# Grams three tiles behind the keys, first gate/up chunks column-tiled, attention state masked one chunk at a time

## The chip, the cores and the metric

The kernel runs on one core of one Trainium2 chip. The metric is the device time of one execution in microseconds (us); lower is better. Three runs of the kernel before gave 291.62, 291.98 and 292.02 us, with a median of 291.98 us. The profile is that of one more execution (291.88 us), whose recorded span is 290.6 us. TensorE had its full clock throughout (granted clock 1.0).

The engines are called as in the profile: PE is TensorE (matmuls), PEld its weight loads, DVE is VectorE, ACT is ScalarE, POOL is GpSimd, SP is SyncE, which here issues transfers.

## The reference

Two branches read the same input x of 2048 tokens by 640 channels, and a gate of one number per token mixes them. Branch A is linear attention with 32 heads of 20 channels and a feature map of two softmaxes; branch B is a gated feed-forward layer of width 1728.

```python
qkv = (x @ wqkv)                                   # then split into q, k, v by head
pq, pk = q @ w_phi, k @ w_phi                      # per head, 20x20
phi_q = concat([softmax(pq), softmax(-pq)])        # 40 features per head
phi_k = concat([softmax(pk), softmax(-pk)])
kv  = einsum("bhsf,bhsd->bhfd", phi_k, v)          # the state: sum over all 2048 tokens
z   = einsum("bhsf->bhf", phi_k)
num = einsum("bhqf,bhfd->bhqd", phi_q, kv)
den = einsum("bhqf,bhf->bhq", phi_q, z)[..., None] + 1e-6
a   = (num / den) @ wo
b   = (gelu(x @ w_gate) * (x @ w_up)) @ w_down
g   = sigmoid((x * gate_w).sum(-1, keepdims=True))
out = g * a + (1 - g) * b
```

## The kernel before

The tokens are handled as 16 tiles of 128 and as 4 blocks of 512. The kernel has two stages.

In the first stage, each tile's values and keys (`vk`, in tiles 4 to 7 the keys alone) are multiplied out into PSUM. ScalarE takes the exponentials (`k_evac`, lines 413 and 416 of the profile), VectorE normalises them into softmaxes (`k_norm`: a sum at line 424, a reciprocal at line 428, two multiplications at line 433), and TensorE then adds the tile's part of the state (`gram`, line 449). Normalised keys lie in a ring of four slots. In between, TensorE multiplies out the queries (`pq`), whose exponentials are at line 516.

TensorE's array can be used as one piece (128 columns of weights) or as two column halves that work side by side. `mm` writes either form, by the flag `self.columns`; line 351 of the profile is the matmul in it. The grams always use the halves.

```python
def mm(self, bank, c0, n, lhs, rhs, first, fin, reads):
    for a, z in ((0, 64), (64, P)) if self.columns else ((0, P),):
        self.sc.op("pe", lambda e: e.matmul(
            self.ps[a:z, bank * 512 + c0:bank * 512 + c0 + n], lhs[:, a:z], rhs, start=first, stop=fin),
            reads=reads, writes=[("ps", bank)], signal=fin and z == P)
...
# end of attention_state (self.columns is True here)
for t in range(4, NT):
    if t < 8:
        self.k_early(t, 1)
    else:
        self.vk(t)
    self.k_norm(t)
    m = 2 * t - 2 if t < 8 else t + 5
    while n < m:
        if n == m - 1:
            for g in range(g, t - 2 if t < 8 else t - 1):
                self.gram(g)
            g = t - 2 if t < 8 else t - 1
        self.pq(order[n][0], order[n][1], n)
        n += 1
```

The second stage is the feed-forward layer with the rest of the attention among it. For a block of 512 tokens, `gateup` makes one of 14 chunks of the hidden layer: five matmuls for the gate into one PSUM bank, five for the up projection into another (line 620), a gelu on ScalarE (line 623), and a product on VectorE (`hT`, line 625), which frees the second bank. Chunks alternate between the bank pairs (0, 1) and (6, 7). The remainder chunk, number 13, packs its 64 gate and 64 up columns into one group of five matmuls (line 630) and uses one bank.

After the first three chunks of the first block come the last two grams. The state is copied out of PSUM (`kv_evac`), turned by a transfer (line 475), and masked to its block-diagonal form by 20 small products on VectorE (`kv_mask`, line 504), after 4 small copies (line 485). `num(t)` then multiplies a tile's queries with the state into banks 2 to 5 (line 653) and divides on VectorE (lines 669 to 680, the last of which read those banks). `down_pair` makes the output projection in steps of two matmuls that use the two row halves of the array (line 710).

```python
def gateups(b, after):
    for idx, c in enumerate([0, 1, 13] + list(range(2, 13))):
        if c == 13:
            self.gateup(b, c, (2,))
        else:
            self.gateup(b, c, pairs[self.pn % 2])
            self.pn += 1
        after(idx)

def downs(b, side):
    ...                      # the steps of down_pair; before step n:
    if n in side:
        self.num(side[n])

def state(idx):
    if idx == 2:
        self.gram(14)
        self.gram(15)
        self.kv_evac()
        self.gates()
    if idx == 6:
        self.kv_mask()

def first_nums(idx):
    if idx in (3, 6, 9, 12):
        self.num(idx // 3 - 1)
...
at = (8, 44, 80, 116)
gateups(0, state)
gateups(1, first_nums)
for b in range(self.NB):
    downs(b, {at[k]: 4 * b + 4 + k for k in range(4)} if b < 3 else {})
    if b < 2:
        gateups(b + 2, none)
```

Waits are placed by a small scheduler: every instruction waits for the last writer and readers of the buffers that it names, and each engine runs its instructions in the order in which the program issues them.

Of the kernel before, what the change touches and what calls it, by code (L numbers as in the profile page):

```python
# [3 lines left out]
P = 128  # L4
# [3 lines left out]
ALU = mybir.AluOpType  # L8
# [99 lines left out]
class _Kernel:  # L108
# [368 lines left out]
            self.Ek[:, 0, :, :].rearrange("p s f -> p (s f)")),  # L477
            reads=[("Ek", 0, 0), ("Ek", 0, 1)], writes=[("Ek", 2, 0), ("Ek", 2, 1)])

    def kv_mask(self):  # L480
        sc = self.sc
        for r in (0, 1):
            for s in (0, 1):
                a, z = 64 * r, 64 * r + 64
                sc.op("dve", lambda e: e.tensor_copy(
                    self.KV[a:z, :, s, :].rearrange("p i (h c) -> p i h c", c=self.DB)[:, :, :, self.DB - 1],
                    self.hmask[a:z, r, :, :]), reads=[("hmask", r)], writes=[("KVd", r, s)])
        self.kvk = {(i, r): [] for i in range(self.KD) for r in (0, 1)}
        lows = {g: lo for g, a, b, c, lo, f0, nf in self.gram_groups()}
        for i in range(self.KD):  # L490
            for r in (0, 1):
                j = 5 * r + i
                a, q = 64 * r, 64 * (j % 2)
                hlo = 16 * r + 3 * i
                for g in range(hlo // 3, (hlo + 3) // 3 + 1):
                    h0, h1 = max(hlo, 3 * g), min(hlo + 3, 3 * g + 2)
                    nh, j0 = h1 - h0 + 1, h0 - hlo
                    o = (j // 2) * P + 64 * (g % 2) + h0 * self.DA - lows[g]
                    dst = self.KV[a:a + 64, i, :, j0 * self.DB:(j0 + nh) * self.DB].rearrange(
                        "p s (h c) -> p s h c", c=self.DB)[:, :, :, 0:self.DA]  # L500
                    src = self.Ek[q:q + 64, 2, :, o:o + nh * self.DA].rearrange("p s (h c) -> p s h c", c=self.DA)
                    m = self.hmask[q:q + 64, j % 2, i, j0:j0 + nh].unsqueeze(1).unsqueeze(3).to_broadcast(
                        [64, 2, nh, self.DA])
                    sc.op("dve", lambda e: e.tensor_tensor(dst, src, m, ALU.mult),  # L504
                          reads=[("Ek", 2, 0), ("hmask", j % 2), ("KVd", r, 0), ("KVd", r, 1)],
                          writes=[("KV", i, r, g)])
                    self.kvk[i, r].append(("KV", i, r, g))

    def pq(self, b, i, n):
        sc = self.sc  # L510
# [19 lines left out]
    def attention_state(self):  # L530
        NT = self.NT
        order = [(b, i) for b in range(self.NB) for i in range(self.KD)]
        sc = self.sc
        sc.op("dve", lambda e: e.memset(self.zero[:, :], 0.0), writes=["zero"])

        def warm(n):
            for i in range(n):
                sc.op("pe", lambda e: e.matmul(self.bank(0), self.zero[:, 0:P], self.zero[:, :], start=True, stop=True),
                      reads=["zero"], writes=[("ps", 0)])
        vs, ve, xt = self.v_step, self.v_first_evac, self.x_transpose  # L540
        warm(7)
        xt(0, 6, "d")
        xt(1, 7, "a")
        xt(2, 2, "d")
        xt(3, 3, "a")
        for t in range(4):
            vs(t, 0)
        for t in range(4):
            vs(t, 1)
        for t in range(4):  # L550
            vs(t, 2)
        for t in range(4):
            vs(t, 3)
        self.blockdiag()
        self.gate_column(6)
        for t in range(4):
            vs(t, 4)
            ve([t], "ad"[t % 2], False)
            if t == 2:
                ve([0, 1, 2], "a", True)  # L560
        ve([3], "d", True)
        f = self.fold
        self.v_early(4, 6)
        self.v_early(5, 0)
        f(0, "k", (2, 3), "d")
        f(1, "k", (4, 5), "a")
        self.v_early(6, 6)
        f(2, "k", (2, 3), "d")
        f(3, "k", (4, 5), "a")
        f(4, "k", (0, 1), "d")  # L570
        self.v_early(7, 6)
        self.k_early(0, 2)
        f(0, "q", (4, 5), "d")
        f(1, "q", (6, 7), "d")
        self.k_early(1, 0)
        f(2, "q", (4, 5), "d")
        f(3, "q", (6, 7), "d")
        self.k_early(2, 2)
        f(4, "q", (4, 5), "d")
        self.k_norm(0)  # L580
        self.k_early(3, 0)
        self.k_norm(1)
        self.pq(0, 1, 1)
        self.pq(0, 0, 0)
        self.pq(0, 3, 3)
        self.columns = True
        self.gram(0)
        self.k_norm(2)
        self.pq(0, 2, 2)
        self.k_norm(3)  # L590
        n = 4
        g = 1
# [6 lines that stand above are left out]
            m = 2 * t - 2 if t < 8 else t + 5  # L599
            while n < m:  # L600
                if n == m - 1:
                    for g in range(g, t - 2 if t < 8 else t - 1):
                        self.gram(g)
                    g = t - 2 if t < 8 else t - 1
                self.pq(order[n][0], order[n][1], n)
                n += 1

    def gateup(self, b, c, banks):
        sc = self.sc
        xs = lambda kt: self.xT[:, kt, b * self.BT:(b + 1) * self.BT]  # L610
        xr = [("xT", t) for t in range(4 * b, 4 * b + 4)]
# [4 lines left out]
        if c < 13:  # L616
            i = 0 if c < 7 else 1
            for w, wk, bk in ((self.wg_sb, "wg", banks[0]), (self.wu_sb, "wu", banks[1])):
                for kt in range(self.KD):
                    sc.op("pe", lambda e, kt=kt, w=w, bk=bk: e.matmul(  # L620
                        self.bank(bk), w[:, kt, c * P:(c + 1) * P], xs(kt), start=(kt == 0), stop=(kt == self.KD - 1)),
                        reads=xr + [(wk, i)], writes=[("ps", bk)], signal=(kt == self.KD - 1))
            sc.op("act", lambda e: e.activation(self.gl[:, slot, :], self.bank(banks[0]), AF.Gelu_apprx_tanh),  # L623
                  reads=[("ps", banks[0])], writes=[("gl", slot)], guard=self.oldw)
            sc.op("dve", lambda e: e.tensor_tensor(hT[:, c, :], self.bank(banks[1]), self.gl[:, slot, :], ALU.mult),  # L625
                  reads=[("ps", banks[1]), ("gl", slot)], writes=[("hT", hk, c)], guard=oldw)
        else:
            bk = banks[0]
            for kt in range(self.KD):
                sc.op("pe", lambda e, kt=kt: e.matmul(  # L630
                    self.bank(bk), self.wgu_sb[:, kt, :], xs(kt), start=(kt == 0), stop=(kt == self.KD - 1)),
                    reads=xr + ["wgu0", "wgu1"], writes=[("ps", bk)], signal=(kt == self.KD - 1))
            sc.op("act", lambda e: e.activation(self.gl[64:128, slot, :], self.ps[0:64, bk * 512:bk * 512 + 512],
                                                AF.Gelu_apprx_tanh),
                  reads=[("ps", bk)], writes=[("gl", slot)], guard=self.oldw)
            for r in (0, 1):
                odd = lambda v: v.rearrange("p (u r q) -> p u r q", r=2, q=P)[:, :, r, :]
                sc.op("dve", lambda e: e.tensor_tensor(
                    odd(hT[64 * r:64 * r + 64, c, :]), odd(self.ps[64:128, bk * 512:bk * 512 + 512]),
                    odd(self.gl[64:128, slot, :]), ALU.mult),  # L640
                    reads=[("ps", bk), ("gl", slot)], writes=[("hT", hk, c, r)], guard=oldw)
# [110 lines left out]
    def ffn(self):  # L752
        self.gn = 0
        self.pn = 0
        self.columns = False
        pairs = [(0, 1), (6, 7)]

        def gateups(b, after):
            for idx, c in enumerate([0, 1, 13] + list(range(2, 13))):
                if c == 13:  # L760
                    self.gateup(b, c, (2,))
                else:
                    self.gateup(b, c, pairs[self.pn % 2])
                    self.pn += 1
                after(idx)

        def downs(b, side):
# [7 lines left out]
                        self.num(side[n])  # L775

        def state(idx):
            if idx == 2:
                self.gram(14)
                self.gram(15)  # L780
                self.kv_evac()
                self.gates()
            if idx == 6:
                self.kv_mask()

        def first_nums(idx):
            if idx in (3, 6, 9, 12):
                self.num(idx // 3 - 1)

        def none(idx):  # L790
            pass
        at = (8, 44, 80, 116)
        gateups(0, state)
        gateups(1, first_nums)
        for b in range(self.NB):
# [47 lines left out]
```

The softmax here doesn't subtract the row's maximum and nothing guards it: scores larger than these inputs give would overflow.

## Time and profile before

| what | value |
|---|---|
| time, median of 3 | 291.98 us |
| span of the profile | 290.6 us |
| gate/up matmuls (line 620) | 506 recorded, 379 ns each as recorded, overlapping |
| down and output projection (line 710) | 1258 recorded, 93.6 us |
| products hT (line 625) | 52, 691 ns each |
| gelu (line 623) | 52, 598 ns each |
| normalising one tile: lines 424, 428, 433 | 1481 + 553 + 2 x 822 ns |
| mask products (line 504) | 20, 189 to 290 ns each |

A line of the waits reads: engine and line that waited, the engine and line whose end released it, then the total in us, how often, and the longest. A line of the timeline reads: start in us, length in us, engine, line, operation, output and inputs, and how many instructions are merged in it; in brackets the idle time of the engine before it and what ended that. Successive matmuls overlap in the records, since their ends are modelled, so the pace of TensorE is read from starts, and a few matmul records are missing.

### The profile page before, as it was taken

How to read it: one execution, taken by the hardware profiler on the slowest of the kernel's cores; microseconds unless marked ns; L12 is line 12 of the kernel's file. 1: busy time of each engine (PE TensorE's matmuls, PEld its weight loads, DVE VectorE, ACT ScalarE, POOL GpSimd, SP SyncE). 2: the span in 40 equal slices, each digit the busy share in tenths (PEclk: the TensorE clock that was granted, in tenths of full speed). 3: DMA queues.
4: the chain of work that ended last, by engine and by line, in shares of the span. 5: the costliest groups of instructions: out<-in, count | busy, mean ns of one | idle time of the engine just before them, and what ended most of it. 6: DMA issues, size and time to landing. Idle time of an engine off the chain costs nothing.

```text
span 290.6 us, 6966 instructions
## 1 busy us (share of the span) xinstructions
PE 282.1 (97%) x2990; PEld 179.2 (62%) x3007; DVE 167.5 (58%) x337; ACT 105.2 (36%) x199; POOL 27.6 (10%) x52
## 2 busy tenths in 40 slices
PE   7999998999999999999999999999999999999996
PEld 3666788699954444444477644447764444777786
DVE  2248999999876742677767533235753323575001
ACT  3367887576673223222202232320223232022021
POOL 7000000000000000011131300001130000113000
PEclk9999999999999999999999999999999999999999
DMA  7999995000002000011114220000322000042211
GB/s 226 198 177 250 367 366 168 0 2 2 2 0 45 2 0 0 3 24 23 25 25 44 74 68 0 0 3 2 52 66 68 0 0 2 2 43 74 68 48 49
DMA packets 36937, 18.66 MB, mean 64 GB/s; under 512 B 28970, under 2 KB 36394, under 8 KB 36906
## 3 DMA queue, kind: packets, MB, share of 16 engines
q1 hardware_dynamic: 36096, 17.86, 25.9%
q8 instruction: 23, 0.38, 0.6%
q10 hardware_dynamic: 810, 0.35, 0.5%
q14 instruction: 8, 0.07, 0.1%
HBM read 9.04 MB, written 2.62 MB: 40 GB/s over the span
## 4 chain that ended last, share of the span: by engine, by line
PE 82%; DVE 8%; SPq 3%; issue 3%; DMA 2%; ACT 2%; ACTq 0%
PE ps L620 36%; PE ps L710 27%; PE ps L351 13%; DVE Dk L424 2%; PE ps L653 2%; DVE Ek L433 2%; DMA xT<-in_A_x_dram 2%; PE ps L630 1%; SPq L220 1%; DVE KV L504 1%; PE ps L449 1%; DVE Dk L428 1%; ACT Ek L413 1%; PE ps L331 1%; SPq L224 1%
## 5 line engine op out<-in xcount | busy, mean ns | idle before, releaser
L625 DVE TENSOR_TENSOR hT<-ps,gl 128x512 bf16<-128x512 f32 x52 | 35.8, 691 | 57.4 <-PE ps L620 56.6
L710 PE MATMUL ps<-wd_sb,hT 64*128 64x320 bf16 (+2 forms) x918 | 66.3, 288 | 0.0
L620 PE MATMUL ps<-xT,wu_sb 128*128 128x512 bf16 x256 | 63.8, 379 | 1.2 <-DVE hT L625 1.0
L620 PE MATMUL ps<-xT,wg_sb 128*128 128x512 bf16 x250 | 62.9, 379 | 1.3 <-issue 1.0
L623 ACT ACTIVATE gl<-ps 128x512 bf16<-128x512 f32 x52 | 31.0, 598 | 72.8 <-PE ps L620 66.3
L710 PEld LDWEIGHTS ps<-wd_sb,hT 64*128 64x128 bf16 x918 | 42.8, 94 | 15.4 <-ACT gl L623 0.8
L682 POOL TENSOR_TENSOR Og<-O,O 128x640 bf16<-128x640 bf16 x16 | 22.3, 1396 | 239.8 <-DVE O L680 239.8
L620 PEld LDWEIGHTS ps<-xT,wu_sb 128*128 128x128 bf16 x260 | 25.4, 98 | 32.0 <-DVE hT L625 1.5
L620 PEld LDWEIGHTS ps<-xT,wg_sb 128*128 128x128 bf16 x260 | 24.8, 98 | 30.1 <-issue 0.9
L723 ACT ACTIVATE outsb<-ps,Gm 128x320 bf16<-128x320 f32 (+2 forms) x31 | 14.6, 516 | 75.3 <-PE ps L710 75.3
L351 PE MATMUL ps<-w,xT 128*64 128x512 bf16 (+6 forms) x398 | 41.4, 325 | 0.2
L351 PEld LDWEIGHTS ps<-w,xT 128*64 128x64 bf16 (+1 forms) x400 | 33.4, 107 | 7.3 <-DMA xT<-in_A_x_dram 0.2
L710 PE MATMUL ps<-wo_sb,goT 64*128 64x320 bf16 (+2 forms) x340 | 27.3, 288 | 0.0
L351 PE MATMUL ps<-xT,wq 128*64 128x512 bf16 (+1 forms) x184 | 25.8, 380 | 0.4 <-ACT Eq L516 0.3
L433 DVE TENSOR_TENSOR Ek<-Ek,Dk 128x640 bf16<-128x640 bf16 x32 | 25.0, 822 | 0.6
L680 DVE TENSOR_TENSOR O<-ps,RH 128x640 bf16<-128x640 f32 x32 | 24.8, 817 | 0.0
L424 DVE TENSOR_REDUCE Dk<-Ek 128x64 f32<-128x1280 bf16 x16 | 23.7, 1481 | 1.5 <-ACT gcol L416 1.5
L516 ACT ACTIVATE Eq<-ps 128x512 bf16<-128x512 f32 x40 | 21.7, 605 | 2.6 <-PE ps L351 2.3
L413 ACT ACTIVATE Ek<-ps 128x640 bf16<-128x640 f32 x32 | 20.8, 704 | 3.5 <-PE ps L351 3.5
L710 PEld LDWEIGHTS ps<-wo_sb,goT 64*128 64x128 bf16 x340 | 16.2, 94 | 5.6
L351 PEld LDWEIGHTS ps<-xT,wq 128*64 128x64 bf16 (+1 forms) x185 | 14.5, 108 | 4.1 <-ACT Eq L516 0.8
L669 DVE RECIPROCAL RH<-ps 128x32 f32<-128x32 f32 x16 | 5.7, 358 | 17.3 <-PE ps L653 17.3
(65 smaller groups left out, 145.6 us busy)
## 6 DMA issues: line engine op xcount, KB each, us to landing
out_dram<-outsb SPq DMA_DIRECT2D x7, 320.0 KB, 2.5
wd_sb<-in_B_w_down_dram SPq DMA_DIRECT2D x1, 2080.0 KB, 13.9
wg_sb<-in_B_w_gate_dram SPq DMA_DIRECT2D x1, 1120.0 KB, 6.0
wu_sb<-in_B_w_up_dram SPq DMA_DIRECT2D x1, 1120.0 KB, 8.5
wg_sb<-in_B_w_gate_dram SPq DMA_DIRECT2D x1, 960.0 KB, 9.6
wu_sb<-in_B_w_up_dram SPq DMA_DIRECT2D x1, 960.0 KB, 10.2
w<-in_A_wqkv_dram SPq DMA_DIRECT2D x5, 160.0 KB, 4.2
wo_sb<-in_A_wo_dram SPq DMA_DIRECT2D x1, 800.0 KB, 9.6
```

The costliest lines, as they stand in the source:

```text
L351: self.sc.op("pe", lambda e: e.matmul(self.ps[a:z, bank * 512 + c0:bank * 512 + c0 + n], lhs[:, a:z], rhs, start=first, stop=fin), reads=r ...
L413: self.sc.op("act", lambda e, s=s, scale=scale: e.activation(self.Ek[:, se, s, :], self.ps[:, o:o + self.D], AF.Exp, scale=scale), reads=[ ...
L424: sc.op("dve", lambda e: e.tensor_reduce(self.Dk[:, se, 0, :].rearrange("p (s h) -> p s h", h=H), self.Ek[:, se, :, :].rearrange("p s (h d ...
L433: sc.op("dve", lambda e, v=v, r=r: e.tensor_tensor(v, v, r, ALU.mult), reads=[("Rk", se)], writes=[("Ek", se, s)])
L516: sc.op("act", lambda e, s=s, scale=scale: e.activation(self.Eq[:, s, i, b * self.BT:(b + 1) * self.BT], self.bank(bank), AF.Exp, scale=sc ...
L620: sc.op("pe", lambda e, kt=kt, w=w, bk=bk: e.matmul(self.bank(bk), w[:, kt, c * P:(c + 1) * P], xs(kt), start=(kt == 0), stop=(kt == self. ...
L623: sc.op("act", lambda e: e.activation(self.gl[:, slot, :], self.bank(banks[0]), AF.Gelu_apprx_tanh), reads=[("ps", banks[0])], writes=[("g ...
L625: sc.op("dve", lambda e: e.tensor_tensor(hT[:, c, :], self.bank(banks[1]), self.gl[:, slot, :], ALU.mult), reads=[("ps", banks[1]), ("gl", ...
L680: dve(lambda e, o=o, f=f, s=s: e.tensor_tensor(o, V[s][:, :, :, 0:DH], f, ALU.mult), rb + [key(6 + s)], [("O", s, sl)], guard=old)
L682: sc.op("pool", lambda e: e.tensor_tensor(self.Og[:, sl, :], self.O1[:, sl, :], self.O2[:, sl, :], ALU.add), reads=[("O", 0, sl), ("O", 1, ...
L710: sc.op("pe", lambda e: e.matmul(self.bank(bk, w), lhs, rhs, start=opens and x == 0, stop=end and not opens, skip_group_check=True), reads ...
L723: sc.op("act", lambda e: e.activation(dst, self.bank(bk, w), AF.Copy, scale=g), reads=rd, writes=wr)
```

## The change

The change has four parts. From tile 8 on, the grams run three tiles behind the keys rather than two, so that TensorE needn't catch VectorE at its normalising; three grams rather than two are then left for the second stage. The gate/up matmuls go through `mm`, and the first three chunks use the column halves, as the grams among them do, so that the form of the array changes less often. The masks are applied for one chunk of the state after each of five gate/up chunks, and no longer all at once. Lastly, the remainder chunk takes a bank of the alternating pairs instead of bank 2, so that the numerators can begin one chunk earlier, and the fifth and sixth numerators move to steps 12 and 46 of the output projection.

```diff
-    def kv_mask(self):
+    def kv_ones(self):
         ...   # the 4 small copies
+
+    def kv_mask(self, i):
         ...
-        for i in range(self.KD):
-            for r in (0, 1):
+        for r in (0, 1):
         ...   # the products of chunk i, as before
@@ attention_state
-                    for g in range(g, t - 2 if t < 8 else t - 1):
+                    for g in range(g, t - 2):
                         self.gram(g)
-                    g = t - 2 if t < 8 else t - 1
+                    g = t - 2
@@ gateup (the remainder chunk likewise)
                 for kt in range(self.KD):
-                    sc.op("pe", lambda e, kt=kt, w=w, bk=bk: e.matmul(
-                        self.bank(bk), w[:, kt, c * P:(c + 1) * P], xs(kt), start=(kt == 0), stop=(kt == self.KD - 1)),
-                        reads=xr + [(wk, i)], writes=[("ps", bk)], signal=(kt == self.KD - 1))
+                    self.mm(bk, 0, 512, w[:, kt, c * P:(c + 1) * P], xs(kt), kt == 0, kt == self.KD - 1, xr + [(wk, i)])
@@ ffn
-        self.columns = False
         pairs = [(0, 1), (6, 7)]
         def gateups(b, after):
             for idx, c in enumerate([0, 1, 13] + list(range(2, 13))):
-                if c == 13:
-                    self.gateup(b, c, (2,))
-                else:
-                    self.gateup(b, c, pairs[self.pn % 2])
-                    self.pn += 1
+                self.gateup(b, c, pairs[self.pn % 2])
+                self.pn += 1
                 after(idx)
         def state(idx):
+            if idx < 3:
+                self.gram(13 + idx)
             if idx == 2:
-                self.gram(14)
-                self.gram(15)
+                self.columns = False
                 self.kv_evac()
                 self.gates()
-            if idx == 6:
-                self.kv_mask()
+                self.kv_ones()
+            if 6 <= idx < 11:
+                self.kv_mask(idx - 6)
         def first_nums(idx):
-            if idx in (3, 6, 9, 12):
-                self.num(idx // 3 - 1)
+            if idx in (2, 5, 8, 11):
+                self.num(idx // 3)
-        at = (8, 44, 80, 116)
+        at = (12, 46, 80, 116)
```

More of the change, by code (lines that the diff above doesn't have):

```diff
@@ L488, in kv_mask @@
         self.kvk = {(i, r): [] for i in range(self.KD) for r in (0, 1)}
+    def kv_mask(self, i):
+        sc = self.sc
         lows = {g: lo for g, a, b, c, lo, f0, nf in self.gram_groups()}
-        for i in range(self.KD):
-            for r in (0, 1):
[L492 to L507, printed above, removed]
@@ new lines, in kv_mask @@
+        for r in (0, 1):
+            j = 5 * r + i
+            a, q = 64 * r, 64 * (j % 2)
+            hlo = 16 * r + 3 * i
+            for g in range(hlo // 3, (hlo + 3) // 3 + 1):
+                h0, h1 = max(hlo, 3 * g), min(hlo + 3, 3 * g + 2)
+                nh, j0 = h1 - h0 + 1, h0 - hlo
+                o = (j // 2) * P + 64 * (g % 2) + h0 * self.DA - lows[g]
+                dst = self.KV[a:a + 64, i, :, j0 * self.DB:(j0 + nh) * self.DB].rearrange(
+                    "p s (h c) -> p s h c", c=self.DB)[:, :, :, 0:self.DA]
+                src = self.Ek[q:q + 64, 2, :, o:o + nh * self.DA].rearrange("p s (h c) -> p s h c", c=self.DA)
+                m = self.hmask[q:q + 64, j % 2, i, j0:j0 + nh].unsqueeze(1).unsqueeze(3).to_broadcast(
+                    [64, 2, nh, self.DA])
+                sc.op("dve", lambda e: e.tensor_tensor(dst, src, m, ALU.mult),
+                      reads=[("Ek", 2, 0), ("hmask", j % 2), ("KVd", r, 0), ("KVd", r, 1)],
+                      writes=[("KV", i, r, g)])
+                self.kvk[i, r].append(("KV", i, r, g))
@@ L629, in gateup @@
             for kt in range(self.KD):
-                sc.op("pe", lambda e, kt=kt: e.matmul(
-                    self.bank(bk), self.wgu_sb[:, kt, :], xs(kt), start=(kt == 0), stop=(kt == self.KD - 1)),
-                    reads=xr + ["wgu0", "wgu1"], writes=[("ps", bk)], signal=(kt == self.KD - 1))
+                self.mm(bk, 0, 512, self.wgu_sb[:, kt, :], xs(kt), kt == 0, kt == self.KD - 1, xr + ["wgu0", "wgu1"])
             sc.op("act", lambda e: e.activation(self.gl[64:128, slot, :], self.ps[0:64, bk * 512:bk * 512 + 512],
```

## The prediction

> **What bounds the kernel now.** I read the page first, for the engine that sets the end: the busy shares, then the chain that ended last.
>
> ```profile
> PE 282.1 (97%) x2990; PEld 179.2 (62%) x3007; DVE 167.5 (58%) x337; ACT 105.2 (36%) x199; POOL 27.6 (10%) x52
> PE 82%; DVE 8%; SPq 3%; issue 3%; DMA 2%; ACT 2%; ACTq 0%
> ```
>
> TensorE is busy 97% of the 290.6 us span. The change leaves its multiplications as they are, so what can be won is its idle time: at most 290.6 - 282.1 = 8.5 us, or 2.9%, and part of that lies in the loads at the start and the tail at the end, which the change doesn't touch. So I went to the list of waits for those in which TensorE waits for VectorE after the start. There are three.
>
> ```profile
> PE ps L449 <- DVE Ek L433: 1.2, 1, 1.2
> PE ps L620 <- DVE hT L625: 1.0, 1, 1.0
> PE ps L653 <- DVE O L680: 0.4, 1, 0.4
> ```
>
> Each occurs once. The three parts of the change aim at these three. The ends of matmuls are modelled and some records are missing, so the idle numbers are too small; I take each loss from starts instead. First the timeline around the wait of the grams (line 449), at the switch from keys alone to values and keys together (tile 8).
>
> ```profile
> 49.14 0.57 PE L449 MATMUL ps<-Ek,vaug 128*64 128x120 bf16 x11
> 49.23 1.56 DVE L433 TENSOR_TENSOR Ek<-Ek,Dk 128x640 bf16<-128x640 bf16 x2
> 50.90 0.46 PE L449 MATMUL ps<-Ek,vaug 128*64 128x120 bf16 x11 [1.19 <-DVE Ek L433]
> 51.19 1.25 PE L351 MATMUL ps<-xT,wq 128*64 128x512 bf16 x10
> 52.27 2.88 PE L351 MATMUL ps<-w,xT 128*64 128x512 bf16 x30
> ```
>
> Gram 5 starts at 49.14; gram 6 follows only at 50.90, when the two multiplications at line 433 that normalise tile 6 are done.
>
> Second, the mask and the first gate/up chunks after it:
>
> ```profile
> 97.34 4.29 DVE L504 TENSOR_TENSOR KV<-Ek,hmask 64x126 bf16<-64x126 bf16 x20
> 100.14 1.24 PE L620 MATMUL ps<-xT,wg_sb 128*128 128x512 bf16 x5
> 101.67 1.29 DVE L625 TENSOR_TENSOR hT<-ps,gl 128x512 bf16<-128x512 f32 x2
> 102.42 1.25 PE L620 MATMUL ps<-xT,wu_sb 128*128 128x512 bf16 x5 [1.03 <-DVE hT L625]
> ```
>
> Twenty mask operations run as one block of 4.29 us; the product hT that frees a PSUM bank stands behind them, and TensorE behind that. Third, numerators 3 and 4:
>
> ```profile
> 143.79 1.26 PE L710 MATMUL ps<-wd_sb,hT 64*128 64x320 bf16 x16
> 143.85 1.55 DVE L680 TENSOR_TENSOR O<-ps,RH 128x640 bf16<-128x640 f32 x2
> 145.46 0.56 PE L653 MATMUL ps<-KV,Eq 64*128 64x88 bf16 x20 [0.41 <-DVE O L680]
> ```
>
> Numerator 4 needs the four banks that the division of numerator 3 (ending with line 680) still reads.
>
> Last, the same view where the shape of the array changes:
>
> ```profile
> 82.06 1.24 PE L620 MATMUL ps<-xT,wu_sb 128*128 128x512 bf16 x5
> 85.30 1.24 PE L630 MATMUL ps<-xT,wgu_sb 128*128 128x512 bf16 x5
> 86.47 0.78 PE L449 MATMUL ps<-Ek,vaug 128*64 128x120 bf16 x22
> 88.27 1.24 PE L620 MATMUL ps<-xT,wu_sb 128*128 128x512 bf16 x5
> ```
>
> A group of five 128x512 matmuls takes 1.08 us from start to start (82.06, 83.14, 84.22, 85.30 in this view). Groups stand as 128*128, the grams as 128*64.
>
> **What the Trainium skill says.** "TensorEngine Tiling (Array Packing)", section Key Properties: "Changing tiling mode (not just tile) drains the TensorE". The trace agrees: 85.30 + 1.08 = 86.38, and the grams start at 86.47, 0.09 us late. The same page, section Feature Incompatibilities, says that column tiling rules out the fast weight load. The trace has 109 ns for a 64-column load and 98 ns for a full one, and the column form needs two. Whether this shows is worked out below. "TensorE: Matmul & The Clock Gate", section Architectural detail, calls ScalarE and VectorE strict first-in-first-out. That is what the second excerpt shows: the product waits behind masks with which it has nothing to do.
>
> **The change part by part.**
>
> *Grams three behind.* From tile 8 on, iteration t runs the grams up to t-3 rather than t-2; tiles below 8 stay. Iteration 8 had grams 5 and 6 and now has 5 alone. In the undisturbed iterations the 30 matmuls of line 351 start 4.07 us apart ((76.68 - 52.27)/6). Iteration 8 starts at 46.43, so iteration 9 could start at 50.50; it starts at 52.27, which is 1.77 late. Of that, 0.28 is the second gram itself, which is only moved; the wait is **1.49 us**. Does it come back later? VectorE takes 3.58 us to normalise a tile (50.71 to 54.29) against TensorE's 4.07, so its backlog shrinks. Tile 7 is done at 54.37; its gram would now run at about 57.2. For tile 15: VectorE, without a gap from 65.03, would start it at 65.03 + 4 x 3.6 = 79.4, and its exponentials end at about 81.16 - 1.77 = 79.4, so it is normalised at about 83.0; its gram is due at about 85. Four key slots suffice, as gram t-3 is issued before the keys of tile t+1 overwrite its slot. I count it whole.
>
> *Gate/up column-tiled.* Grams 13, 14 and 15 now follow the first three gate/up groups, with all these in 128*64 form. There were three changes of form: the first group starts at 82.06 - 1.08 = 80.98, where the queries (79.66 + 1.08, and 0.05 for two gram matmuls among them) would end at 80.79, so 0.19; then 0.09; then 88.27 - 1.08 = 87.19 against 86.47 + 2 x 0.28 = 87.03, so 0.16. One change remains, at 0.16 to 0.19: **0.26 us** won. Against this stand five groups of ten half-width matmuls rather than five whole ones. In the value/key loop, ten column pairs of 512 and five of 257 take 76.68 to 79.39 = 2.71 us; at the pitch of whole matmuls (1.08/5 = 0.216, and 0.108 for 257) that makes 2.70. So a pair costs what a whole matmul costs, and the loads stay hidden: 0.
>
> *Masks split.* The group at 100.14 should be followed by the next at 101.22; it is at 102.42: **1.20 us**. Now the small copies (0.68 us) go ahead of chunk 3 and four masks (4.29/5 = 0.86) behind each of five chunks. With the product (0.69) that is 1.55 of 2.16 us per chunk, so nothing piles up. The transpose that the masks read is issued at 90.52 and lands after 3.4; it stays ahead of the first mask by over 2 us.
>
> *Numerators one chunk earlier, numerator 4 at step 12 instead of 8.* A pair of steps' matmuls takes 4.89/36 = 0.136 us, so 8 steps from 143.79 end at 144.88; numerator 4 starts at 145.46: 0.58 us lost, which goes. But the remainder group (chunk 13) now takes a bank of the rotating pairs and numerator 0 follows it directly. Counting from numerator 0's start N: that group's gelu (0.59) and two products (0.88) are done at N+1.7, the division (3.53) at N+5.2, the next chunk's product at N+5.95; TensorE wants that bank at N+0.49+5x1.08 = N+5.9. About 0.1 lost. At the far end the first down-projection wants a bank at N+4.9 after numerator 3, and its product is done at N+5.1: 0.2 lost. Net **0.28 us**.
>
> Sum: 1.49 + 0.26 + 1.20 + 0.28 = 3.2 us, all on TensorE, which has no other wait to fall into: 291.98 - 3.2 = **288.8 us**, a ratio of 1.011.
>
> **Rivals.**
> 1. *Another wait takes the place of the first.* If VectorE's backlog still meets the grams, at gram 15 or at the first products hT (which stand behind the normalisation of tile 15), the 1.49 us shrink to perhaps 0.3: 290.0 us. For it: VectorE is busy 26.39 of the 28 us from 51 to 79, and the first two products run only after about 83.0. Against it: the banks they free are wanted at 86.6 at the earliest.
> 2. *Column-tiled groups cost more.* If the weight loads showed, twenty-five pairs at 10 to 40 ns each would add 0.3 to 1 us: 289.1 to 289.8. If pairs did not overlap at all, 5.4 us: 294. Against it stands the 2.71 us above, for the same shapes.
> 3. *Numerators collide.* If each of the four divisions delayed a product by 0.3 us more than I count, 1.2 us go back: 290.0. For it: numerator 0 is now behind the remainder group, and my slack there is about nothing. Against it: from numerator 1 on, the three whole chunks between two numerators are as before, with 0.86 us to spare (product done at 124.83, bank wanted at 125.69).
> 4. *Nothing comes through*, because something later sets the end: 292. Against it: from 146 to the end TensorE is at work without a gap worth naming, so an earlier start is an earlier end.
>
> **Range and chances.** The two large terms, 2.7 us, are read from starts and have room behind them; the rest is small either way. Half of rival 1 or all of rival 3 gives 289.6 to 290; if my two small losses don't appear, 288.5. Range 288.2 to 289.8. Faster by over 2% needs 286.1 us, which asks for almost twice what the touched waits hold; slower by over 2% needs 297.8. Both 1 in 100.
>
> **What would show it.** In the profile after: the wait of line 449 for line 433 is gone, and iterations 8 and 9 are 4.07 us apart; the groups and grams from about 79 to 85.4 stand in 128*64 form, with groups 1.08 us apart and 0.28 added per gram; the wait of the gate/up matmuls for hT is under 0.3 us; numerator 4 has no wait; masks appear as five blocks of four. I am wrong if a gate/up group in column form takes more than 1.1 us, if a gram waits for VectorE near 85, or if gaps of more than 0.3 us stand behind the numerators in the second gate/up block.

## The result and the profile after

The changed kernel takes 289.28 us (median of 4 runs, 288.68 to 289.97) against 292.00 us for the kernel before (median of 4, 291.62 to 292.67): a ratio of 0.9905, interval 0.9876 to 0.9935. It is 2.7 us faster (the interval allows 1.9 to 3.6). The prediction said 288.8 us, within 288.2 to 289.8.

The page of the changed kernel, busy shares and the chain that ended last:

```profile
PE 284.0 (98%) x3032; PEld 190.1 (66%) x3032; DVE 166.7 (58%) x337; ACT 105.1 (36%) x199; POOL 27.6 (10%) x52
PE 97%; DMA 1%; ACT 1%; issue 0%; ACTq 0%
```

The chain ran through VectorE for 8% of the span before; now VectorE isn't in it, and TensorE makes up 97% of it. The gate/up matmuls have moved to line 351, the output projection to line 708, the numerators to 651 with their division at 667 to 678, the masks to 506. The list of waits of the changed kernel no longer has TensorE behind the normalisation (line 433) or behind the division, and behind a product hT it has only a weight load:

```profile
PEld ps L351 <- DVE hT L625: 0.4, 1, 0.4
```

The timelines at the places shown for the kernel before. First tile 8, with one gram and no wait:

```profile
47.06 2.98 PE L351 MATMUL ps<-w,xT 128*64 128x512 bf16 x30
49.77 0.48 PE L449 MATMUL ps<-Ek,vaug 128*64 128x120 bf16 x9
50.05 0.40 PE L351 MATMUL ps<-xT,wq 128*64 128x512 bf16 x1
50.09 0.25 PE L449 MATMUL ps<-Ek,vaug 128*64 128x120 bf16 x2
51.15 2.98 PE L351 MATMUL ps<-w,xT 128*64 128x512 bf16 x30
```

Tile 9's values and keys start 4.09 us after tile 8's; it was 5.84. Next the first gate/up groups, now in halves (128*64), and the one change of form that is left:

```profile
79.75 1.35 PE L351 MATMUL ps<-xT,wg_sb 128*64 128x512 bf16 x10
80.83 1.35 PE L351 MATMUL ps<-xT,wu_sb 128*64 128x512 bf16 x10
81.91 0.48 PE L449 MATMUL ps<-Ek,vaug 128*64 128x120 bf16 x9
82.19 0.40 PE L351 MATMUL ps<-xT,wg_sb 128*64 128x512 bf16 x1
...
85.75 0.57 PE L449 MATMUL ps<-Ek,vaug 128*64 128x120 bf16 x11
86.25 1.25 PE L351 MATMUL ps<-xT,wg_sb 128*128 128x512 bf16 x5
```

Groups of ten halves start 1.08 us apart like groups of five whole ones, a gram adds 0.28, and from 86.03 (85.75 + 0.28) to 86.25, 0.22 us are lost where the form changes. Then the masks, in fours behind each product:

```profile
95.09 0.69 DVE L625 TENSOR_TENSOR hT<-ps,gl 128x512 bf16<-128x512 f32 x1 [1.47 <-PE ps L351]
95.70 0.82 DVE L506 TENSOR_TENSOR KV<-Ek,hmask 64x126 bf16<-64x126 bf16 x4
97.05 1.24 PE L351 MATMUL ps<-xT,wg_sb 128*128 128x512 bf16 x5
98.13 1.24 PE L351 MATMUL ps<-xT,wu_sb 128*128 128x512 bf16 x5
```

**A measure that scatters less.** Single executions start and end unevenly. The stretch from the first value matmul of tile 8 to the last small group of matmuls (the start of its row in the timeline) leaves both ends out, and the change lies inside it. Before, it runs from 46.43 to 288.01 = 241.58 us; after, from 47.06 to 285.48 = 238.42 us. So the change wins **3.16 us** there (3.2 predicted). The profiled execution came to tile 8 later by 0.63 us, and its end, after the last matmuls, took 3.22 us rather than 2.59. Together these make the 1.9 us by which the spans differ (290.6 and 288.7). The stretch comes from one execution of each kernel. But in the three variants below in which TensorE should find nothing more to wait for than in the changed kernel (2, 7 and 11) it was 238.42, 238.42 and 238.43 us, so it tells a tenth of a microsecond, where the intervals of the ratios reach 0.4 to 1.1 us to either side.

By stage: to the gate/up group after the last gram 1.56 us were won (46.43 to 87.18 against 47.06 to 86.25), from there to the second block 1.21 (to the group at 112.14 and 110.00), and from there to the third block 0.4.

### The profile page after: what moved, and what is told of

It reads as the page before. It is cut to its first block, busy times and chain, and to the rows that moved or that the text cites. A ratio compares the mean times of both kernels' runs of the same rounds, so it can differ in the third digit from the quotient of the medians.

```text
span 288.7 us, 7036 instructions
## 1 busy us (share of the span) xinstructions
PE 284.0 (98%) x3032; PEld 190.1 (66%) x3032; DVE 166.7 (58%) x337; ACT 105.1 (36%) x199; POOL 27.6 (10%) x52
## 4 chain that ended last, share of the span: by engine, by line
PE 97%; DMA 1%; ACT 1%; issue 0%; ACTq 0%
PE ps L351 61%; PE ps L708 28%; PE ps L651 2%; PE ps L363 2%; PE ps L449 2%; DMA xtok<-in_A_x_dram 1%; PE ps L331 1%; PE ps L290 1%; ACT Ek L413 0%; ACT Eq L518 0%; ACT outsb L721 0%; ACT gcol L416 0%; PE ps L313 0%; ACTq L42 0%
## 5 line engine op out<-in xcount | busy, mean ns | idle before, releaser
L708 PE MATMUL ps<-wd_sb,hT 64*128 64x320 bf16 (+2 forms) x918 | 67.6, 288 | 0.0
L351 PE MATMUL ps<-xT,wg_sb 128*128 128x512 bf16 (+1 forms) x270 | 64.9, 379 | 0.0
L351 PE MATMUL ps<-xT,wu_sb 128*128 128x512 bf16 (+1 forms) x270 | 64.8, 379 | 0.0
L708 PEld LDWEIGHTS ps<-wd_sb,hT 64*128 64x128 bf16 x918 | 46.0, 94 | 13.2 <-ACT gl L623 0.8
L351 PEld LDWEIGHTS ps<-xT,wu_sb 128*128 128x128 bf16 (+1 forms) x270 | 26.5, 99 | 29.7 <-DVE hT L625 0.4
L351 PEld LDWEIGHTS ps<-xT,wg_sb 128*128 128x128 bf16 (+1 forms) x270 | 25.9, 99 | 28.7 <-issue 0.5
L351 PEld LDWEIGHTS ps<-w,xT 128*64 128x64 bf16 (+1 forms) x400 | 35.9, 107 | 4.7
L708 PE MATMUL ps<-wo_sb,goT 64*128 64x320 bf16 (+2 forms) x340 | 28.2, 288 | 0.0
L708 PEld LDWEIGHTS ps<-wo_sb,goT 64*128 64x128 bf16 x340 | 17.7, 94 | 4.7
L351 PEld LDWEIGHTS ps<-xT,wq 128*64 128x64 bf16 (+1 forms) x185 | 15.3, 108 | 3.5 <-ACT Eq L518 0.8
```

The lines of the kernel that those rows point to most:

```text
L351: self.sc.op("pe", lambda e: e.matmul(self.ps[a:z, bank * 512 + c0:bank * 512 + c0 + n], lhs[:, a:z], rhs, start=first, stop=fin), reads=r ...
L708: sc.op("pe", lambda e: e.matmul(self.bank(bk, w), lhs, rhs, start=opens and x == 0, stop=end and not opens, skip_group_check=True), reads ...
```

## The experiments

"The stretch" is the one just named. Each variant was also timed beside the kernel before (whose median was 292.0 to 292.3 us); the variant's median follows in brackets, with the ratio to the kernel before and its 95% interval. Line numbers are those of each variant. In the cuts, "..." stands for lines left out.

**1. Grams two tiles behind again.**

```diff
-                    for g in range(g, t - 2):
+                    for g in range(g, t - 2 if t < 8 else t - 1):
...                                   # g is set likewise
-            if idx < 3:
+            if idx in (1, 2):
                 self.gram(13 + idx)
```

> The new kernel with the grams two tiles behind again from tile 8 on (two grams are then left for the gate/up chunks). Theory A, the wait of gram 6 is worth what the starts show and nothing later gives it back: 1.5 us slower than the new kernel, about 290.8 us, and 5.8 us between the value matmuls of tiles 8 and 9 rather than 4.1. Rival, most of the wait is absorbed later by the backlog of VectorE (first products behind the last normalisation): under 0.4 us slower, about 289.6 us.

In its timeline, the wait is back:

```profile
49.64 0.52 PE L449 MATMUL ps<-Ek,vaug 128*64 128x120 bf16 x10
51.33 0.46 PE L449 MATMUL ps<-Ek,vaug 128*64 128x120 bf16 x11 [1.17 <-DVE Ek L433]
```

The stretch is 239.75 us, 1.33 more than the new kernel's (290.28 us; 0.9947, 0.9926 to 0.9969). Tiles 8 and 9 are 5.83 us apart, that is 1.46 us of wait and 0.28 of moved gram. The rival falls. The last 0.1 us does come back: after the wait, the next iterations are 4.05 us apart, and from the fourth on 4.09 (the kernel before has 4.04 to 4.06, then 4.08 to 4.09).

**2. Three behind, but two again from tile 13.**

```diff
+                    for g in range(g, t - 2 if t < 13 else t - 1):
...                                   # g is set likewise, and the gate/up chunks have two grams, as in 1
```

> The new kernel, three tiles behind up to tile 12 and two behind again from tile 13 on. Theory A1, the wait comes from VectorE's backlog at tile 8, which has shrunk by tile 13 (it is through with tile 11 about 1 us before its gram would be due): no wait of a gram for the normalisation, time as the new kernel, 289.3 us. Rival A2, two tiles are too few wherever the distance changes, as that iteration runs two grams: a wait of over 1 us at tile 13 and 290.5 us.

Its timeline at tile 13, where two grams stand together:

```profile
67.75 2.98 PE L351 MATMUL ps<-w,xT 128*64 128x512 bf16 x30
70.45 0.78 PE L449 MATMUL ps<-Ek,vaug 128*64 128x120 bf16 x20
71.03 0.40 PE L351 MATMUL ps<-xT,wq 128*64 128x512 bf16 x1
72.13 2.87 PE L351 MATMUL ps<-w,xT 128*64 128x512 bf16 x29
```

The iteration takes 4.38 us: 4.09 and a gram. No wait; the stretch is 238.42 us, as the new kernel's (289.71 us; 0.9917, 0.9899 to 0.9935). The normalisation of tile 11, which the second gram needs, ended at 69.47, a microsecond before the two grams began. So the distance of two as such does not make the wait. It takes VectorE's backlog at tile 8: in the kernel before, tile 6 was done only at 50.79 (49.23 + 1.56), when TensorE had already been waiting for it.

**3. The distance alone, on the kernel before.** The grams as in the new kernel, grams 13, 14 and 15 together behind the third gate/up chunk.

```diff
...                                   # range(g, t - 2), as in the new kernel
             if idx == 2:
+                self.gram(13)
                 self.gram(14)
```

> The kernel before with only the grams three tiles behind; three grams stand together behind the third gate/up chunk. Theory A, the parts add up on their own: 1.5 us faster than before, 290.5 us, with the waits at the masks (1.2 us) and at numerator 4 (0.6 us) as before. Rival, the parts need one another (an earlier TensorE waits the longer at the masks, as their transfer and VectorE come no earlier): under 0.5 us faster, over 291.5 us, and a longer wait at the masks.

The stretch is 240.25 us, 1.33 less than before (290.92 us; 0.9957, 0.9943 to 0.9971). From its list of waits:

```profile
PEld ps L620 <- DVE hT L625: 1.5, 1, 1.5
PE ps L620 <- DVE hT L625: 1.0, 1, 1.0
PE ps L653 <- DVE O L680: 0.4, 1, 0.4
```

Both other waits are as large as before: an earlier TensorE doesn't wait longer at the masks. This part gives the same 1.33 us alone as on top of the others (experiment 1).

**4. All masks at once, the small copies early.**

```diff
-            if 6 <= idx < 11:
-                self.kv_mask(idx - 6)
+            if idx == 6:
+                for i in range(self.KD):
+                    self.kv_mask(i)
```

> The new kernel with all 20 mask products after the seventh gate/up chunk again, but the four small copies left where the new kernel has them. Theory C, the block on VectorE is hidden up to a fixed slack (4.97 us of copies and masks cost 1.20 us, so 3.77 us are hidden): 4.29 us of masks alone cost 0.5 us, about 289.8 us. Rival, the split of the masks alone makes the gain: the whole 1.2 us come back, 290.5 us.

```profile
95.27 4.28 DVE L506 TENSOR_TENSOR KV<-Ek,hmask 64x126 bf16<-64x126 bf16 x20
98.78 1.24 PE L351 MATMUL ps<-xT,wg_sb 128*128 128x512 bf16 x5
99.58 1.29 DVE L625 TENSOR_TENSOR hT<-ps,gl 128x512 bf16<-128x512 f32 x2
100.33 1.25 PE L351 MATMUL ps<-xT,wu_sb 128*128 128x512 bf16 x5 [0.31 <-DVE hT L625]
```

From start to start 1.55 us rather than 1.08: 0.47 lost, and the stretch is 238.92 us, 0.50 more (289.73 us; 0.9921, 0.9897 to 0.9944).

**5. Masks and copies at once.**

```diff
+            if idx == 6:
                 self.kv_ones()
-            if 6 <= idx < 11:
-                self.kv_mask(idx - 6)
+                for i in range(self.KD):
+                    self.kv_mask(i)
```

> The new kernel with both the four small copies and the 20 masks in one block after the seventh gate/up chunk, as before. Theory C, 3.77 us of such a block are hidden: 4.97 us cost 1.2 us from start to start, about 290.5 us. Rival, the copies' own 0.7 us lie in a gap of VectorE: 0.5 us, as with the masks alone, 289.8 us.

```profile
94.75 0.68 DVE L485 COPY KV<-hmask 64x20 bf16<-64x20 bf16 x4
95.46 4.29 DVE L506 TENSOR_TENSOR KV<-Ek,hmask 64x126 bf16<-64x126 bf16 x20
98.26 1.24 PE L351 MATMUL ps<-xT,wg_sb 128*128 128x512 bf16 x5
99.78 1.29 DVE L625 TENSOR_TENSOR hT<-ps,gl 128x512 bf16<-128x512 f32 x2
100.52 1.25 PE L351 MATMUL ps<-xT,wu_sb 128*128 128x512 bf16 x5 [1.02 <-DVE hT L625]
```

The stretch is 239.61 us, 1.19 more (290.56 us; 0.9954, 0.9941 to 0.9966). In this order, moving the four copies away (0.68 us on VectorE) wins 0.69 of the 1.19 us and splitting the masks then the other 0.50. Between these two lengths of the block, 0.68 us more cost 0.69 us, and in both about 3.8 us were hidden. The order matters to the shares: four masks and the copies together would be a block of about 1.5 us (0.68 + 4.28/5), an estimate far below 3.8, so splitting the masks alone should have won all of it. No run has that.

**6. All gate/up groups whole.** The three grams among them stay in halves, so there are seven changes of form rather than one.

```diff
+        self.columns = False          # before the gate/up chunks, not after the third
```

> The new kernel with all gate/up groups in whole form; the three grams among the first chunks stay in halves, so there are seven changes of form rather than one. Theory B, a change to halves costs about 0.09 and one back about 0.2 us, while the halves themselves cost nothing: 3 x 0.09 + 3 x 0.2 = 0.9 us more up to the third chunk, about 290.2 us. Rival, the halves cost something too (ten weight loads of 109 ns rather than five of 98 for a group), which cancels it: under 0.3 us more.

The stretch is 239.09 us, 0.67 more (289.49 us; 0.9907, 0.9879 to 0.9935; the time alone wouldn't tell it). Six more changes of form for 0.67 us is 0.11 each on average, less than I had expected. The rival, under 0.3, falls.

**7. All gate/up groups of all blocks in halves.**

```diff
             if idx == 2:
-                self.columns = False
```

> The new kernel with all gate/up groups of all four blocks in column halves, 540 pairs of matmuls rather than 25 of them. Theory B, a pair of halves takes just what a whole matmul takes: within 0.3 us of the new kernel, 289.0 to 289.6 us, and groups 1.08 us apart in every block. Rival, the second weight load shows with 2 to 10 ns a pair: 1 to 5 us slower, 290.3 to 294.5 us.

From its groups with shapes kept apart (count, then busy time and mean ns of one):

```profile
L351 PE MATMUL ps<-xT,wg_sb 128*64 128x512 bf16 x520 | 65.4, 380 | 0.0
L351 PEld LDWEIGHTS ps<-xT,wu_sb 128*64 128x64 bf16 x520 | 31.4, 110 | 24.8 <-DVE hT L625 0.4
```

The stretch is 238.42 us, as the new kernel's (289.03 us; 0.9905, 0.9869 to 0.9941). One change of form is saved as well, worth about 0.1, so 515 more pairs cost some 0.1 us: 0.2 ns a pair. The third block, which has no numerators among its groups, says the same: from its first group to the output projection it takes 29.27 us here (162.63 to 191.90) and 29.25 in the new kernel (163.62 to 192.87), for 135 pairs or whole matmuls. A half's weight load takes 110 ns (98 for a whole one), and there are twice as many, all hidden behind 512-column matmuls.

**8. Halves in every second chunk of the last two blocks.** That makes 26 more changes of form: 13 within each block. The expectation counted 14, but the last chunk of a block is in halves, and from there to the row halves of the output projection is a change that the new kernel has too.

```diff
+                if b >= 2:
+                    self.columns = idx % 2 == 1
                 self.gateup(b, c, pairs[self.pn % 2])
```

> The new kernel, but in the third and fourth block every second gate/up chunk in column halves, which makes 28 changes of form that were not there. Theory B, 0.09 us to halves and 0.2 us back, 0.29 us for two: 14 x 0.29 = 4.1 us more, about 293.4 us. Rival, the 0.2 us seen at the one change left are an accident of that place (grams before it): under 1.5 us more.

```profile
164.38 1.24 PE L351 MATMUL ps<-xT,wu_sb 128*128 128x512 bf16 x5
165.55 1.27 PE L351 MATMUL ps<-xT,wg_sb 128*64 128x512 bf16 x10
166.66 1.25 PE L351 MATMUL ps<-xT,wu_sb 128*64 128x512 bf16 x10
167.83 1.25 PE L351 MATMUL ps<-xT,wgu_sb 128*128 128x512 bf16 x5
```

The stretch is 241.39 us, 2.97 more: 0.114 us a change (291.97 us; 0.9986, 0.9973 to 1.0). It lies between the two expectations. The rows show why my 4.1 was too much: 1.17 where the form changes, in either direction, against 1.08, so 0.09 each way, and some 0.02 in the first group after it. I had carried over 0.2 us for the way back from a place where grams went before, and counted two changes too many.

**9. Numerators where they were.**

```diff
-            if idx in (2, 5, 8, 11):
-                self.num(idx // 3)
+            if idx in (3, 6, 9, 12):
+                self.num(idx // 3 - 1)
...
-        at = (12, 46, 80, 116)
+        at = (8, 44, 80, 116)
```

> The new kernel with the numerators where they were (after chunks 3, 6, 9 and 12 of the second block, then before steps 8 and 44). Theory D, numerator 4 waits again for the division of numerator 3: 0.6 us, less the 0.1 us that numerator 0 costs behind the remainder chunk: 0.5 us more, 289.8 us, with the wait at line 651 back. Rival, the bank pairs, which the remainder chunk now takes part in, have changed what numerator 4 meets: no wait, same time.

```profile
141.40 1.26 PE L708 MATMUL ps<-wd_sb,hT 64*128 64x320 bf16 x16
143.06 0.57 PE L651 MATMUL ps<-KV,Eq 64*128 64x88 bf16 x20 [0.41 <-DVE O L678]
```

The wait is back, and the stretch is 238.82 us, 0.40 more (290.20 us; 0.9929, 0.9903 to 0.9955).

**10 and 11. One of the two moves undone.** Variant 10 takes the first half of that diff alone (chunks 3, 6, 9, 12), variant 11 the second half alone (steps 8 and 44).

> The new kernel with the first numerators after chunks 3, 6, 9 and 12 again, but numerator 4 at step 12 and 5 at step 46 as in the new kernel. Theory D1, either of the two moves removes the wait of numerator 4 on its own, this one barely (the division of numerator 3 ended 1.62 us after the first step, step 12 ends after 1.63): no or under 0.1 us of wait, time as the new kernel. Rival, both moves are needed: 0.3 us or more of wait.

> The new kernel with numerators 4 and 5 at steps 8 and 44 again, but the first ones a chunk earlier as in the new kernel. Theory D1, this move alone removes the wait (it puts 2.2 us more between numerators 3 and 4 than before, and 0.6 us were lacking): no wait, time as the new kernel. Rival, both moves are needed: 0.3 us or more of wait.

Variant 10: 238.28 us, 0.14 less than the new kernel (289.38 us; 0.9913, 0.9892 to 0.9934); behind the division only a weight load waits, 0.2 us. Variant 11: 238.43 us (289.20 us; 0.9903, 0.9885 to 0.9921), no wait for the division. Either move is enough. The one that puts numerators a chunk earlier is the worse of the two, for it has a cost of its own, seen below.

**12. Only two numerators in the second block.** The rest move two places on, into the output projections.

```diff
-            if idx in (2, 5, 8, 11):
-                self.num(idx // 3)
+            if idx in (5, 9):
+                self.num((idx - 5) // 4)
...
-        at = (12, 46, 80, 116)
+        at = (2, 36, 80, 116)
-            downs(b, {at[k]: 4 * b + 4 + k for k in range(4)} if b < 3 else {})
+            downs(b, {at[k]: 4 * b + 2 + k for k in range(4) if 4 * b + 2 + k < self.NT})
```

> The new kernel with only numerators 0 and 1 among the gate/up chunks of the second block (after chunks 5 and 9); all others are two places later, in the output projections, whose array form they share: steps 2, 36, 80 and 116 of each, the last two in the fourth. Theory B, a numerator among gate/up chunks costs a change of form there and back, 0.21 us: two fewer win 0.4 us, about 288.9 us, 238.0 us from the value matmuls of tile 8 to the last matmul rather than 238.4. Rival, the later numerators run into the output projection (turned output not there when its last steps want it, or the banks of the last pair still read): no gain or slower.

Slower than both kernels: 294.25 us; 1.0078, 1.0062 to 1.0095; the stretch is 243.05 us, 4.63 more. Up to the first output projection it was as theory B has it: from tile 8 to there 93.38 us (46.57 to 139.95) against 94.68 (47.06 to 141.74), so 1.30 less, of which 0.78 are the two numerators moved on (0.39 each) and 0.52 are won. But the rival holds for what follows. Its list of waits has a new entry, and the timeline shows one case of it:

```profile
PEld ps L708 <- DMA goT<-Og: 5.6, 5, 1.7
PE ps L708 <- DMA goT<-Og: 4.0, 5, 1.4
```

```profile
272.62 0.57 PE L651 MATMUL ps<-KV,Eq 64*128 64x88 bf16 x17
275.54 1.55 DVE L678 TENSOR_TENSOR O<-ps,RH 128x640 bf16<-128x640 f32 x2
277.22 1.39 POOL L680 TENSOR_TENSOR Og<-O,O 128x640 bf16<-128x640 bf16 x1 [5.16 <-DVE O L678]
281.32 0.72 PE L708 MATMUL ps<-wo_sb,goT 64*128 64x256 bf16 x9 [1.33 <-DMA goT<-Og]
```

From a numerator's matmuls to its turned output 8.7 us pass (272.62 to 281.32). The 52 steps left between them, from step 36 to 88, end after 7.1 us (279.70), and TensorE stands for the rest. After the start of the first output projection the variant takes 149.67 us against 143.74, so with the 0.78 us of moved work taken off it loses 5.15. No version measured here is clearly better than the new kernel.

## Why the prediction was right

The time lies in the range, and the terms of the sum can be set beside what undoing each part costs on the stretch:

| term | predicted | measured |
|---|---|---|
| grams three behind | 1.49 | 1.33 (experiments 1 and 3): a wait of 1.46, less 0.1 in slower iterations |
| form of the array | 0.26 | 0.23: experiment 3 against the new kernel, see below |
| masks and copies | 1.20 | 1.19 (5) |
| numerators, net | 0.28 | 0.40 (9) |
| sum | 3.2 | 3.15 by parts, 3.16 directly |

*Grams.* The step held: the wait goes whole, and VectorE's backlog takes nothing back. In the changed kernel's list of waits no gram stands behind the normalisation, and tile 15's normalisation ended at 83.86 (82.30 + 1.56), before its gram at 85.75. What I missed is small: iterations right after a wait run 4.05 us apart and later ones 4.09, so the pitch of 4.07 was a mean over both, and removing the wait costs 0.1 us again.

*Form.* The mechanism held, and so did "a pair costs what a whole matmul costs", tested over 540 pairs (7). Up to the grams' end, experiment 3 differs from the changed kernel in form alone: from tile 8 to the up group behind the last gram it takes 40.51 us (47.19 to 87.70), and the changed kernel 40.28 (47.06 to 87.34). The prediction's 0.26 is a little too much because the one change that is left costs 0.22 and not 0.16 to 0.19. Between gate/up groups a change costs 0.11 in either direction (8); why the way back after a gram costs more (0.14 in experiment 6, 0.22 here) was not tried.

*Masks.* The best of the terms, since it was read from start to start and not from the idle time (1.03 us) that the list of waits gave. Experiments 4 and 5 add that the loss is the length of the block beyond some 3.8 us, so taking the four small copies out of it would have won 0.69 by itself.

*Numerators.* The 0.58 us of the wait went: from the first step of the output projection to the first matmul of line 708 with wo, 2.89 us before and 2.30 after (144.04 - 141.74). Of the 0.3 us of new losses that I set against it, about 0.2 came: up to the output projection 0.09 (27.42 us from the second block's remainder group against 27.33 in variant 10), where the group at 121.47 followed 1.15 rather than 1.08 us after the one before it, as predicted (0.1); and 0.11 in the first output projection. The last step's number, 0.2, was too large, as I had put the product's end at N+5.1 and it came at N+4.97 (136.82 to 141.79).

Rival 1 is ruled out by experiments 1 and 3, rival 2 by 7, and rival 4 by the 3.16 us. Rival 3, losses beyond the 0.3 us counted, did not happen: 0.2 us came in all.

The measured 2.7 us are less than the 3.16 of the stretch, and the difference is within the interval. In the profiled executions it lies in the start and the end, which the prediction took as unchanged ("an earlier start is an earlier end").

At the start, in the changed kernel's profile, the 20 transposes of the first tokens took 314 ns each (minimum, median and maximum below), and in the profile before 219:

```profile
L290 PE MATMUL ps<-ident,xtok x20: 288/314/314, 4.7 to 6.7; 128*128 128x128 bf16 x20
```

They follow one another every 107 ns there, and every 56 ns in the profile before. In the profile of experiment 6 the first ten start some 107 ns apart and the last ten 56. The granted clock in the profiles is 1.0 throughout and doesn't show this, but such a halving of the pace looks like a matmul clock that came up later in some executions. The Trainium skill says as much ("TensorE: Matmul & The Clock Gate", section What's actually happening): the window that frees the clock runs freely, so where it falls in a kernel's start differs from run to run. It can explain a part of the scatter only. Tile 8 began anywhere from 46.11 to 47.31 us in the variants, and in 1 and 4, where all 20 transposes were fast, still at 46.87 and 46.62.

At the end there is a cost that the prediction missed. From the last small group of matmuls to the end of the span 2.59 us passed before and 3.22 after. The page has a queue that fetches instructions, with 23 transfers before and 24 after:

```profile
q8 instruction: 23, 0.38, 0.6%
q8 instruction: 24, 0.39, 0.6%
```

The last of them starts at 286.38 us in the changed kernel, 0.90 us after that last group, while the final outputs are written. The last two of these writes take 3.0 and 2.3 us from issue to landing, where they took 1.8 and 1.6. So it is in all ten profiles in which a fetch falls behind the last group: their ends take 3.07 to 3.38 us. In the other four it comes earlier, and the end takes 2.59 (before), 2.66 (3), 2.59 (6) and 2.88 us (8, where it starts 0.3 us ahead of the group). The changed program is longer (7036 recorded instructions against 6966), so the late fetch most likely belongs to it, and about 0.6 of the 3.16 us is given back. It also fits that experiment 6, at 0.67 us more on the stretch, has a median only 0.2 us higher. No run moved the fetch alone.

## What to carry to other kernels

When one engine is busy 97% of the time, list the waits in which it stands behind another, and size each from start to start against the undisturbed pitch. Here these sizes added up (3.15 by parts, 3.16 together), and the idle times in the list were too small (1.03 us for a loss of 1.19). The block of small operations on VectorE was free up to a slack of 3.8 us and cost what it had beyond that, so it should be enough to bring such a block below its slack, by moving some of it or by splitting it (here both were done). When work is moved later to save something local, count the whole chain to its consumer, with transfers: experiment 12 won 0.5 us and lost 5. And look at how the program ends: a gain on the busiest engine can be given back in part behind its last instruction.

## What was not expected

- A change between the whole array and its column halves costs 0.11 us in either direction between gate/up groups (0.114 over 26 changes), and a pair of column halves of 512 costs what a whole matmul costs, to 0.2 ns, although its weight loads are twice as many and slower (110 against 98 ns).
- The two halves of the array can drift apart. In the changed kernel the first output projection has to wait with one row half for a product (done at 141.79) and not with the other: the halves start at 141.74 and 141.85, where in variant 10 they start 3 ns apart. They stay 110 ns apart to the end of that projection (163.28 and 163.39). The merged row of 24 matmuls lasts 1.91 us where it lasts 1.80 in variant 10, and 0.11 us more are needed to the third block (23.91 against 23.80 us from the first matmul with wo to the remainder group). The column halves do the same at the grams, which have 11 matmuls, an odd number for two halves: in the kernel before they start 4 ns apart after the wait (51.19) and 40 ns apart after the next gram (55.24); in the changed kernel, where iterations take 4.09 us rather than 4.05, they start 106 to 110 ns apart. That the drift is what costs the 0.11 us, and the 0.04 us per iteration of experiment 1, fits all these numbers but wasn't tried alone.
